# A written-out instruction order with another rule for VectorE's masks, other ranks, and one weight load split (DeltaNet, then a mixture of experts)

## The chip, the cores and the metric

The kernel runs on one core of one Trainium2 chip. The metric is the device time of one launch in microseconds (us). Three runs of the kernel before gave 531.04, 532.78 and 533.56 us, the median is 532.78 us.

## What is computed

The first half is DeltaNet attention: 4 batches of 8 heads, 768 steps, 48 features. The second half sends each of the 3072 rows of the result (384 features) to one of 8 experts. Cut to what matters:

```python
k_n = k / (norm(k) + 1e-6)
for t in range(S):                                # S = 768
    y[:, :, t] = q_t @ state                      # the state before the step
    v_old = k_t @ state
    state += beta_t * outer(k_t, v_t - v_old)
x = y.transpose(0, 2, 1, 3).reshape(B * S, H * D)
logits = x @ w_gate                               # 8 experts
expert = argmax(logits); gate = softmax(logits)[expert]
out = gate * (relu(x @ w1[expert]) @ w2[expert])  # w1 384x1024, w2 1024x384
```

## The kernel before

The time steps are cut into 12 tiles of 64 steps. Inside a tile the recurrence is solved at once: products of keys with keys and queries with keys (`scores`), an inverse of a triangular matrix per head (`invert`, one for each pair of tiles, numbers 0 to 5), and a chain on TensorE that carries the state on (`turn`). In detail:

- `scores(t)` runs 32 or 64 small matmuls into a PSUM pair, ScalarE copies the results to `XY` and to `Pm(t)`. Then VectorE multiplies `Pm(t)` by a fixed 0/1 pattern (L412, 128x1024). This multiplication is called the mask of tile t here. For tiles 0 and 1 the diagonal blocks `GD` are copied straight from PSUM in four quarters each (L311 on VectorE, L309 on ScalarE); later tiles get theirs by a DMA.
- `invert(n)` is VectorE's work: two block transposes (L437), a chain of some 17 tiny operations of 32 columns that forms the norms (L445 to L470, each needs the one before), one scaling (L476), 16 elimination steps (L486 to L498), a first transpose back (L517), 16 more steps (L504, L509) and a second transpose back (L517). It serves tiles 2n and 2n+1.
- `turn(t)` takes the values scaled by the norms, applies the inverse twice (L583, with L593 between) and makes the next state (L607). TensorE and ScalarE take turns in it: each matmul group waits for a ScalarE copy of the one before. `output(t)` adds the state's part (L554) and the masked part (L639, this needs the mask of tile t), `logits(t)` transposes the result and multiplies it by the gate's weights (L659, L669, L678).
- `route(m, part)` does the argmax, the softmax and the counting for a group of row tiles. The groups are row tiles 0-7, 8-15, 16-17, 18-21 and 22-23. Its part 1 begins with `rk` (L752), which reads a count made by TensorE (L743, L747), and has `su` (L766), which reads an exponential from ScalarE (L722).
- `listed` makes the lists of rows per expert for tiles 0-17, then 18-21, then 22-23: VectorE builds comparisons (L796, L800, L804), TensorE multiplies them (L812), one more matmul (L817) and a copy give `lst` (L821). From it `numbered` makes `rows_ei`. GpSimd then gathers 256 early rows of expert 0 (L886), TensorE transposes them (L927), and the first expert matmul (L945) begins with 256 rows.
- The experts follow one another: `turned_rows` (L927), `hidden` (L945), `second` (L977), with a short matmul for a remainder (L1025). Weights are loaded by SyncE's queue in order, three 512 KB parts of w1 and two 768 KB parts of w2 for each expert (`weights`).

The order of instructions on each engine isn't the order of the code. Every piece of work is handed to `Plan.op` with its engine, an assumed cost, what it reads and writes, and a rank (`prio`; smaller is more urgent). `Plan.order` walks through time with these assumed costs: on each engine that comes free it picks the ready piece with the smallest rank, and waits for a piece of rank -70 or less if that comes ready within the time of the one picked. It also places filler matmuls (L1120) into pauses of TensorE [...], as many as `ENOUGH` allows in a window. What comes out is one fixed list per engine, run in order. The constants at the head of the file are ranks and assumed costs: `RUN` for scores, `OUT`, `LOG`, `LATER`, `OUTL` for outputs and logits, `LISTS`, `L3`, `L4` for the lists, `VP` for the scaling of values (L530), `MASK` for the masks. An inverse n has rank 2n - 4 (number 0: -80), the mask of tile t has rank t - MASK.

Of the kernel before, what the change touches and what calls it, by code (L numbers as in the profile page):

```python
# [20 lines left out]
NT = S // C  # L21
# [7 lines left out]
NK = DM // 128  # L29
# [4 lines left out]
FAR = 1 << 20  # L34
RING = 6
AHEAD = 5
RUN = 4.75
PAGE, FILL, STALL = 125, 3.8, 0.8
OUT, LOG = 1.1, 0.2
LATER, OUTL = 8, 1.3  # L40
LISTS, L3, L4, TURN = 9.5, 20.2, 11.05, 11.0
APART = 5
VP, MASK = 0.5, 2.2
WINDOW, WAKE, STAY, PASS = 3.413, 1600, 1750, 8.5
FILLER, ENOUGH, FROM = 0.22, 2500, 36.0
SLACK = 2.0
URGENT = -70


class Plan:  # L50
# [37 lines left out]
    def order(self):  # L88
        n = len(self.ops)
        self.all = list(self.ops)  # L90
        recent, emptied, fills, last = [], {}, [], False
        users = [[] for _ in range(n)]
        left = [len(o[3]) for o in self.ops]
        for i, o in enumerate(self.ops):
            for d, lat in o[3]:
                users[d].append((i, lat))
        ready = [0.0] * n
        free = {}
        wait = {}
        page, filled = 0, 0.0  # L100
        window, used, fast = 0, {}, False
        for i, o in enumerate(self.ops):
            if not left[i]:
                wait.setdefault(o[0], []).append(i)
        start, fin = [0.0] * n, [0.0] * n
        done = 0

        def stall(j, t):

            cost, passes = self.ops[j][1], self.ops[j][5]  # L110
            if page + passes < PAGE or not passes:
                return 0.0
            return max(0.0, filled - t - cost / passes * (PAGE - page))

        while done < n:
            best = None
            for e, lst in wait.items():
                if not lst:
                    continue
                f = free.get(e, 0.0)  # L120
                t = max(f, min(ready[i] for i in lst))
                if best is None or t < best[0]:
                    best = (t, e)
            t, e = best
            lst = wait[e]
            i = min(
                (j for j in lst if ready[j] <= t + 1e-9),
                key=lambda j: (self.ops[j][4] + STALL * stall(j, t), j),
            )

            soon = [j for j in lst if self.ops[j][4] <= URGENT and t < ready[j] < t + self.ops[i][1] - 0.05]
            if soon and self.ops[i][4] > URGENT:
                i = min(soon, key=lambda j: ready[j])
                t = ready[i]
            lst.remove(i)
            eng, cost, _, _, _, passes, _, use, cold, pairs = self.ops[i]
            start[i] = t

            f = free.get("PE", 0.0)
            last |= 30 < self.ops[i][4] < 90  # L140
            while eng == "PE" and not last and FROM < f < t - FILLER - 0.05:
                recent = [x for x in recent if x[0] > f - WINDOW]
                b = [b for b in (1, 2) if emptied.get(b, 0.0) <= f]
                if not b or sum(x[1] for x in recent) >= ENOUGH:
                    break
                fills.append((f, len(self.all)))
                self.all.append(("PE", FILLER, self.filler(b[0]), [], 99.0, 2, None, 256, 2.0, {b[0]}))
                recent.append((f, 273))
                w = int(f / WINDOW)
                used[w] = used.get(w, 0.0) + 273  # L150
                page = (page + 2) % PAGE
                f += FILLER
            if passes:
                recent.append((t, use + PASS * passes))
            if passes:

                while int(t / WINDOW) > window:
                    fast = used.get(window, 0.0) >= (STAY if fast else WAKE)
                    window += 1
                if not fast:  # L160
                    cost *= cold
                for k in range(8):
                    w = int((t + cost * k / 8) / WINDOW)
                    used[w] = used.get(w, 0.0) + (use + PASS * passes) / 8
            end = t
            if passes:
                each = cost / passes
                while passes:
                    k = min(passes, PAGE - page)
                    end += k * each  # L170
                    passes -= k
                    page += k
                    if page == PAGE:
                        page = 0
                        end = max(end, filled)
                        filled = end + FILL
            else:
                end += cost
            free[e] = fin[i] = end
            if e != "PE":  # L180
                for b in pairs:
                    emptied[b] = max(emptied.get(b, 0.0), end + self.LAT[e])
            done += 1
            for u, lat in users[i]:
                ready[u] = max(ready[u], end + lat)
                left[u] -= 1
                if not left[u]:
                    wait.setdefault(self.ops[u][0], []).append(u)
        self.start, self.fin = start + [t for t, _ in fills], fin + [t + FILLER for t, _ in fills]
        return [i for _, i in sorted([(start[i], i) for i in range(n)] + fills)]  # L190
# [28 lines left out]
def tile_kernel(ctx: ExitStack, tc: tile.TileContext, kq, ktok, vtok, betal, wgk, w1, w2, out):  # L219
    nc = tc.nc  # L220
    P = Plan()
# [8 lines left out]
    fc, where = _consts()  # L230
# [31 lines left out]
    def kb(b):  # L262
        return [("bk", b), ("bk", b + 1)]
# [23 lines left out]
    GD = blk(8)  # L287
# [7 lines left out]
    def dma(eng, o, i):  # L295
        return lambda: eng.dma_start(out=o, in_=i)
# [19 lines left out]
    P.op("DVE", 0.1, lambda: nc.vector.memset(tiny[:], 0.0), w=["tiny"], prio=-99)  # L316
    P.op("ACT", 0.2, lambda: nc.scalar.activation(out=tiny[:], in_=tiny[:], func=AF.Copy), w=["tiny"], prio=-45)
    P.op("ACT", 0.5, dma(nc.scalar, bl[:], betal), w=["bl"], prio=-49, lat=2.5)
    P.op("ACT", 0.5, dma(nc.scalar, cf[:], nc.inline_tensor(fc, name="c_f32").ap()), w=["cf"], prio=-48, lat=2.5)
    P.op("DVE", 0.2, lambda: nc.vector.memset(wg[:], 0.0), w=["wg"], prio=-48)  # L320
    P.op("ACT", 0.5, dma(nc.scalar, wg[:, :, 0:E], wgk), w=["wg"], prio=-40, lat=2.5)
    P.op("DVE", 1.0, lambda: nc.vector.memset(pairs[0][:], 0.0), w=kb(BS), prio=-50)
# [40 lines left out]
    def scores(t):  # L363
# [16 lines left out]
        if t < 2:  # L380
# [1 line left out]
            P.op("PE", 1.15, lambda: run(b, (0,), range(FQ)), r=kKQ(t, (0,)), w=kb(b), prio=t - 95, passes=64, use=770)  # L382

            for q in range(4):
                eng = ("ACT", "DVE")[u]
                o = GD[quad(q), :, 16 * u : 16 * u + 16].rearrange("p c (e f) -> p c e f", e=2)
                i = pairs[b // 2][quad(q)].rearrange("p e (f c) -> p c e f", c=C)[:, 32 * (q % 2) : 32 * (q % 2) + 32]
                P.op(eng, 0.5 if u == 0 else 0.6, copy(eng, o, i), r=kb(b), w=[("GD", q, u, e) for e in range(2)], prio=t - 94)
            P.op("ACT", 1.0, copy(
                "ACT",  # L390
                xy[:, :, 16 * u : 16 * u + 16].rearrange("p c (e f) -> p c e f", e=2),
# [446 lines left out]
            a[:, NK * F :].rearrange("p (c d) -> p c d", c=NF),  # L838
        )

    def weights(e, pr, behind=()):
        i = e % 3
        a1, a2 = wview(i)
        extra = []
        if e == 0:
            extra = kXY(0) + kXY(1) + [("GL", k) for k in range(2)]
        if e == 1:
            extra = [("P", k) for k in range(RING)]
        if e == 2:
            extra = [k for i in range(2) for k in (("U", i), ("U", i, 21))] + [("GD", q, u, e) for q in range(4) for u in range(2) for e in range(2)] + kXY(2)  # L850
            extra += [("TT", k, h) for k in range(2) for h in range(2)]
        for s in range(NK):
            P.op("SP", SP(524288),
                 dma(nc.sync, a1[:, s, :], w1[e].rearrange("(s p) f -> p s f", p=128)[:, s, :]),
                 r=behind, w=[("w", i, s)] + extra, prio=pr + s)
        for h in range(2):
            P.op("SP", SP(786432),
                 dma(nc.sync, a2[:, 4 * h : 4 * h + 4, :],
                     w2[e].rearrange("(c p) d -> p c d", p=128)[:, 4 * h : 4 * h + 4, :]),
                 r=behind, w=[("w", i, 3 + h)] + extra, prio=pr + 3 + h)  # L860
# [128 lines left out]

    def early_rows():  # L990

        weights(0, 8)
        prepare(0)
        two_tiles = lst[:].rearrange("p (t e) o -> p t e o", e=E)[:, 0:2, 0, :]
        numbered(rows_ei[:], two_tiles[:, :, 0], "rows_ei", ["lst"], -74)
        dve(2, lambda: nc.vector.tensor_copy(out=rows_e[:], in_=two_tiles[:, :, 1]), ["lst"], ["rows_e"], -73)
        xv = XIN[0][0]
        for t in range(2):
            P.op("POOL", 1.0, lambda t=t: gather(xv[:, t * DM : t * DM + DM], rows_ei[:, t : t + 1]),
                 r=["rows_ei"] + [("xs", i) for i in range(18)], w=[("xin", 0, t)], prio=11, lat=2.5)  # L1000
# [87 lines left out]
                last_rows()  # L1088
    prepare(1)
    numbered(rows_i[:], lst[:, :, 0], "rows_i", ["lst"], -74)  # L1090
    early()

    weights(1, 20, ["rows_i"])
# [125 lines left out]
```

## Time and profile before

| what | value |
|---|---|
| median of three runs | 532.78 us |
| the profiled execution's own time | 526.99 us |
| its span, first to last instruction | 525.2 us |
| TensorE busy | 468.0 us (89%), mean granted clock 0.952 |
| VectorE busy | 243.7 us (46%) |
| ScalarE busy | 191.0 us (36%) |
| GpSimd busy | 84.9 us (16%) |

The profile is of one execution, and its time lies 5.79 us under the median of the runs. In rows of the timeline the columns are start, duration, engine, line of the code, operation, tiles out<-in, and in brackets the idle time before it and what ended it. A row of windows gives for each engine the busy microseconds, then the granted clock of TensorE as a share of full speed, the DMA share and GB/s. The share of busy time hides that the launch has two halves. In the first, up to about 220 us, VectorE is busy nearly all the time until 186 us. In the second, TensorE is.

### The profile page before, as it was taken

What the parts mean: (1) busy time and instruction counts of PE and PEld (TensorE: products, weight loads), DVE (VectorE), ACT (ScalarE), POOL (GpSimd) and SP (SyncE); (2) the same over time, 40 slices, a digit from 0 to 9 for tenths busy, and PEclk for the clock granted to TensorE, in tenths of its full rate; (3) what the DMA queues carried; (4) which work ended last, traced back from release to release, by engine and by line L of the source; (5) the groups of instructions that cost most, each with busy time, mean ns of one, the idle gap of its engine ahead of it and who ended that gap; (6) DMA issues with size and microseconds to landing.
All of it is one profiled execution on the core that took longest, in us unless ns stands there. A gap on an engine that the chain in (4) does not pass through costs nothing. (4 is left out here: it accounts for less than half of the span.)

```text
span 525.2 us, 15838 instructions
## 1 busy us (share of the span) xinstructions
PE 468.0 (89%) x6850; PEld 321.4 (61%) x6851; DVE 243.7 (46%) x958; ACT 191.0 (36%) x452; POOL 84.9 (16%) x91
## 2 busy tenths in 40 slices
PE   5668898888897898999999999999999999999991
PEld 3557787776786786875755555555555555555550
DVE  3999989999699973251303012212030220121210
ACT  2494978888569974510110110010100111100100
POOL 9100000000010010006510321402301302011020
PEclk9556999899999999999999999999999999999996
DMA  8987365364342434395543413612532301000000
GB/s 202 222 211 201 118 164 161 94 150 131 101 134 94 134 115 152 100 385 176 177 175 121 150 54 139 193 34 107 196 120 82 126 4 46 0 18 30 0 31 13
DMA packets 27849, 63.84 MB, mean 122 GB/s; under 512 B 4026, under 2 KB 16220, under 8 KB 27744
## 3 DMA queue, kind: packets, MB, share of 16 engines
q1 hardware_dynamic: 23376, 52.44, 32.9%
q0 software_dynamic: 3584, 9.44, 5.5%
q10 hardware_dynamic: 816, 0.92, 0.8%
q8 instruction: 54, 0.88, 0.7%
q14 instruction: 19, 0.16, 0.1%
HBM read 49.67 MB, written 11.01 MB: 116 GB/s over the span
## 5 line engine op out<-in xcount | busy, mean ns | idle before, releaser
L945 PE MATMUL pair<-kqA,blkA 128*128 128x416 f32 (+2 forms) x288 | 86.9, 458 | 0.0
L977 PE MATMUL pair<-blkA,kqA 128*128 128x384 f32 x240 | 79.0, 489 | 0.0
L951 DVE TENSOR_SCALAR kqA<-pair 128x416 f32<-128x416 f32 (+2 forms) x36 | 19.6, 543 | 121.7 <-PE pair L945 121.7
L945 PEld LDWEIGHTS pair<-kqA,blkA 128*128 128x128 f32 x288 | 51.2, 190 | 31.3 <-issue 28.3
L977 PEld LDWEIGHTS pair<-blkA,kqA 128*128 128x128 f32 x240 | 45.1, 190 | 33.3 <-issue 3.1
L893 POOL DMA_INDIRECT out<-y,rows_i x30 | 28.7, 956 | 199.7 <-DVE y L1038 122.1
L954 ACT ACTIVATE kqA<-pair 128x416 f32<-128x416 f32 (+2 forms) x36 | 17.2, 478 | 108.9 <-PE pair L945 108.9
L968 ACT ACTIVATE y<-pair,lst 128x384 f32<-128x384 f32 x15 | 8.7, 581 | 128.0 <-PE pair L977 118.3
L373 PE MATMUL pair<-kqA 48*64 48x128 f32 (+1 forms) x896 | 36.3, 319 | 17.4 <-ACT blkA L309 6.0
L945 PE MATMUL pair<-kqA,pA 128*128 128x416 f32 x144 | 51.0, 513 | 0.0
L530 ACT ACTIVATE v<-v,nt 128x48 f32<-128x48 f32 x192 | 48.9, 329 | 3.4 <-DMA v<-in_vtok 1.9
L977 PE MATMUL pair<-pA,kqA 128*128 128x384 f32 x144 | 47.2, 488 | 0.0
L373 PEld LDWEIGHTS pair<-kqA 48*64 48x64 f32 x896 | 29.9, 176 | 23.4 <-ACT pA L309 7.9
L554 PE MATMUL pair<-S,kqA 112*64 112x96 f32 x704 | 35.7, 253 | 9.5 <-ACT S L309 3.1
L945 PEld LDWEIGHTS pair<-kqA,pA 128*128 128x128 f32 x144 | 27.1, 190 | 22.5 <-issue 21.6
L977 PEld LDWEIGHTS pair<-pA,kqA 128*128 128x128 f32 x144 | 27.1, 190 | 20.1 <-issue 1.9
L554 PEld LDWEIGHTS pair<-S,kqA 112*64 112x64 f32 x704 | 30.8, 138 | 12.5 <-issue 4.7
L886 POOL DMA_INDIRECT kqA<-xs,rows_i x30 | 29.8, 994 | 43.2 <-DVE more L1115 26.7
L583 PE MATMUL pair<-R,blkA 32*32 32x48 f32 x1536 | 28.6, 226 | 3.0 <-ACT R L309 1.8
L965 DVE TENSOR_SCALAR y<-pair,lst 128x384 f32<-128x384 f32 x7 | 4.3, 618 | 55.3 <-PE pair L977 55.3
L583 PEld LDWEIGHTS pair<-R,blkA 32*32 32x32 f32 x1536 | 25.3, 146 | 7.3 <-ACT R L309 3.8
L490 DVE TENSOR_TENSOR prod<-blkA 128x16 f32<-128x16 f32 (+7 forms) x96 | 28.8, 300 | 0.0
(136 smaller groups left out, 615.6 us busy)
## 6 DMA issues: line engine op xcount, KB each, us to landing
kqA<-in_kq SPq DMA_DIRECT2D x46, 192.0 KB, 5.2
blkA<-in_w SPq DMA_DIRECT2D x15, 512.0 KB, 4.9
blkA<-in_w SPq DMA_DIRECT2D x10, 768.0 KB, 5.5
v<-in_vtok SPq DMA_DIRECT2D x12, 384.0 KB, 4.1
kt<-in_ktok SPq DMA_DIRECT2D x12, 384.0 KB, 3.6
xs<-x SPq DMA_DIRECT2D x12, 384.0 KB, 2.9
pA<-in_w SPq DMA_DIRECT2D x9, 512.0 KB, 5.6
pA<-in_w SPq DMA_DIRECT2D x6, 768.0 KB, 4.7
```

Of the source, the lines that this page charges most:

```text
L373: nc.tensor.matmul(bk[bank + e][half(x), i * w : i * w + w].rearrange("p (k c) -> p k c", c=C), lhsT=v[feat(e), 0, x * FQ + f, :], rhs=v[f ...
L490: dve(16 * w, lambda j=j, w=w, pl=pl: nc.vector.tensor_tensor(out=pl, in0=gl[:, 16:32, j : j + 1].to_broadcast([128, 16, w]), in1=u[:, j : ...
L530: P.op("ACT", 0.225, lambda v=v, i=i: nc.scalar.activation(out=v, in_=v, func=AF.Copy, scale=nt[:, 16 * u + i : 16 * u + i + 1]), r=[("nt" ...
L554: nc.tensor.matmul(bk[bank + g][half(x ^ g if first else x), 2 * D * i : 2 * D * i + 2 * D], lhsT=KQ(t)[0 : 64 + D, k, x * FQ + f, :], rhs ...
L583: nc.tensor.matmul(at(BZ, f, e)[quad(q)], lhsT=tt[quad(q), :, 16 * u + 8 * e + f], rhs=R[quad(q), f, e, :], start=True, stop=True, skip_gr ...
L886: nc.gpsimd.indirect_dma_start(out=dst, out_offset=None, in_=xs, in_offset=bass.IndirectOffsetOnAxis(ap=idx, axis=0), bounds_check=N - 1, ...
L893: nc.gpsimd.indirect_dma_start(out=out, out_offset=bass.IndirectOffsetOnAxis(ap=idx, axis=0), in_=src, in_offset=None, bounds_check=N - 1, ...
L945: nc.tensor.matmul(bk[b][:, 0:n], lhsT=a1[:, s, f * 128 : f * 128 + 128], rhs=xT[:, s, :], start=(s == 0), stop=(s == NK - 1))
L951: (lambda f=f, b=b: nc.vector.tensor_scalar(out=hT[:, f, :], in0=bk[b][:, 0:n], scalar1=0.0, scalar2=None, op0=OP.max))
L954: (lambda f=f, b=b: nc.scalar.activation(out=hT[:, f, :], in_=bk[b][:, 0:n], func=AF.Relu)),
L968: (lambda: nc.scalar.activation(out=y[0:n], in_=bk[b][0:n, 0:DM], func=AF.Copy, scale=gate)),
L977: nc.tensor.matmul(bk[b][:, 0:DM], lhsT=hT[:, f, at : at + 128], rhs=a2[:, f, :], start=(f == 0), stop=(f == NF - 1))
```

## The change

Six things change; the parts that only move line numbers are left out. In `Plan.order` a rule is added for VectorE: before the piece picked is begun, a piece that is more urgent by over 0.5 and comes ready within `NEAR` (0.3 us, and within the piece's own cost) is waited for. Ranks and `ENOUGH` are changed. The constants' load is told to the planner as landing after 8.5 us in place of 2.5 us. One of the four copies of `GD` for tile 1 moves from VectorE to ScalarE. The two w2 loads of expert 0 are handed over later, with rank 18 to 19 behind the last tile's second result. The order is then made anew from all this, so that pieces not named here also change places.

```diff
-RUN = 4.75
+RUN = 4.5
-OUT, LOG = 1.1, 0.2
-LATER, OUTL = 8, 1.3
-LISTS, L3, L4, TURN = 9.5, 20.2, 11.05, 11.0
+OUT, LOG = 0.6, 0.9
+LATER, OUTL = 7, 1.1
+LISTS, L3, L4, TURN = 10.4, 11.0, 11.05, 11.0
-VP, MASK = 0.5, 2.2
+VP, MASK = 1.5, 1.5
-FILLER, ENOUGH, FROM = 0.22, 2500, 36.0
-SLACK = 2.0
+FILLER, ENOUGH, FROM = 0.22, 2300, 36.0
+NEAR, SLACK = 0.3, 2.0
...
+            elif e == "DVE":
+
+                soon = [j for j in lst if self.ops[j][4] < self.ops[i][4] - 0.5
+                        and t < ready[j] < t + min(self.ops[i][1] - 0.05, NEAR)]
+                if soon:
+                    i = min(soon, key=lambda j: (self.ops[j][4], ready[j]))
+                    t = ready[i]
...
-    P.op("ACT", 0.5, dma(nc.scalar, cf[:], nc.inline_tensor(fc, name="c_f32").ap()), w=["cf"], prio=-48, lat=2.5)
+    P.op("ACT", 0.5, dma(nc.scalar, cf[:], nc.inline_tensor(fc, name="c_f32").ap()), w=["cf"], prio=-48, lat=8.5)
...
-                eng = ("ACT", "DVE")[u]
+                eng = "ACT" if u == 0 or q == 3 else "DVE"
...
-                P.op(eng, 0.5 if u == 0 else 0.6, copy(eng, o, i), r=kb(b), w=[("GD", q, u, e) for e in range(2)], prio=t - 94)
+                P.op(eng, 0.6 if eng == "ACT" else 0.7, copy(eng, o, i), r=kb(b), w=[("GD", q, u, e) for e in range(2)], prio=t - 94)
...
-    def weights(e, pr, behind=()):
+    def weights(e, pr, behind=(), of=(0, 1)):
...
-        for s in range(NK):
+        for s in range(NK if 0 in of else 0):
...
-        for h in range(2):
+        for h in range(2 if 1 in of else 0):
...
-        weights(0, 8)
+        weights(0, 8, of=(0,))
...
+    weights(0, 18, [("Z", (NT - 1) % 2)], (1,))
```

## Prediction

> **What bounds the kernel now.** The page names the last chain only for its final 6 us, so I read the slices of the span first, then windows, then each engine's timeline from the start, looking for the place where the second half begins.
>
> ```profile
> DVE  3999989999699973251303012212030220121210
> 350.00:400.00 50.00, 50.00 (x180) 27.67 (x180) 9.05 (x15) 5.25 (x10) 9.79 (x10) 1.00 0.35 123
> 450.00:500.00 50.00, 49.32 (x174) 26.79 (x173) 10.44 (x18) 4.78 (x9) 3.78 (x4) 1.00 0.04 13
> ```
>
> From the first expert matmul at 219.72 us TensorE is nearly full at full clock: between there and 513 us its idle pieces are 0.98, 0.39, 0.84, 1.18, 1.18 and 0.68 us, 5.3 us in all. Its order and work there are kept by the change but for a few swaps in the first 17 us. So the end moves with the start of that matmul. Ahead of it VectorE is 90% full up to 186 us. It matters where its inverses begin and end:
>
> ```profile
> 10.71 0.22 ACT L309 ACTIVATE ents<-cf 128x24 f32<-128x24 f32 x1 [6.54 <-DMA cf<-c_f]
> 13.24 1.30 DVE L437 STREAM_TRANSPOSE blkA<-blkA 128x512 f32<-128x512 f32 x2 [2.14 <-ACT blkA L309]
> 39.20 0.71 DVE L517 STREAM_TRANSPOSE blkA<-blkA 128x512 f32<-128x512 f32 x1
> 72.21 0.70 DVE L517 STREAM_TRANSPOSE blkA<-blkA 128x512 f32<-128x512 f32 x1
> 136.50 0.22 DVE L766 TENSOR_REDUCE su<-ex 128x8 f32<-128x64 f32 x1 [4.82 <-ACT ex L722]
> 185.49 0.71 DVE L517 STREAM_TRANSPOSE blkA<-blkA 128x512 f32<-128x512 f32 x1
> 193.40 0.55 DVE L796 TENSOR_TENSOR ones_p<-cf,places_f 128x384 f32<-128x384 f32 x1
> ```
>
> ScalarE stands 6.54 us for the constants, with the copies that the first inverse needs behind it. Inverse 0 runs from 13.24 to 39.91, inverse 1 ends at 72.91 and inverse 5 at 186.20. The list begins at 193.40. VectorE stood 4.82 us in the middle of inverse 4. The last stretch decides when the experts begin:
>
> ```profile
> 206.82 0.43 PE L817 MATMUL pair<-cf,lstT 128*128 128x64 f32 x2
> 208.81 1.19 POOL L886 DMA_INDIRECT kqA<-xs,rows_ei  x1 [13.61 <-DVE rows_ei L830]
> 215.65 0.63 PE L927 MATMUL pair<-cf,kqA 128*128 128x128 f32 x4
> 219.72 1.56 PE L945 MATMUL pair<-kqA,blkA 128*128 128x256 f32 x6
> ```
>
> The list's last matmul to the first expert matmul is 12.9 us: list, gather, transposes, with the last turn beside it.
>
> [...] a 128x32 operation is 0.19 us, a 128x256 one 0.42, and in a chain the next starts 0.22 to 0.24 us after the last. [...] Here the clock is 0.50 in 96 to 98 us after four thin microseconds, and 64 matmuls of L583 take 1.51 us instead of 1.13. [...] The early gathers here land 3.5 us after issue. [...] L465 took 1.09 us beside a GpSimd memset where it takes 0.18 later; I let that stand, since both move forward together.
>
> **The change, part by part.** I compared the order of instructions on each engine with the order before.
>
> *Start.* The copy of the constants now stands behind the five quarter copies on ScalarE. Those need 5 x 0.58 us from about 6.9, so they end at 9.8. VectorE keeps three of its four copies of 0.70 us from 8.31 and ends at 10.4. The first transpose goes at 10.45 instead of 13.24: -2.8 us. The cover for the moved quarter is ScalarE, idle there before; without it VectorE would end at 11.1.
>
> *Inverses.* An inverse alone costs 39.91 - 13.24 - 0.9 (the L465 case) = 25.8 us. A mask costs 1.11 to 1.18 us start to start, 2.3 for two. The order now reads: inverse 0, masks 0 to 2, inverses 1 and 2, masks 3 and 4, inverse 3, masks 5 and 6, inverse 4, masks 7 and 8, inverse 5, masks 9 and 10, route group 1 with mask 11 inside, group 2, lists. Before, masks 0 to 5 (7.2 us) all lay in or ahead of inverse 1. Ends, in us: inverse 0 at 37.1 (39.91 before), 1 at 37.1 + 3.4 + 25.8 = 66.3 (72.91), 2 at 92.1, 3 at 120.2. Group 0's first 14 small operations stay alternated with inverse 4's chain: 14 such pairs took 3.39 us, 0.24 a pair, hardly more than the chain alone; all of group 0 adds 1.2. So inverse 4 ends at 120.2 + 2.3 + 25.8 + 1.2 = 149.5 plus its waits.
>
> *The wait in inverse 4.* The 4.82 us stall was for an exponential that ScalarE did late. Now the exponential is still behind turn 6's first copies, and `rk` stands only 8 operations behind `su`, where 25 inverse operations lay between. `rk` needs TensorE's count, which before ended 1.0 us ahead of turn 6 (139.99 against 140.99). VectorE gets there at about 129.5. Turn 6 by the turn chain: turn 2 at 67 instead of 77.27, turn 3 at 80.3 (13.3 later, as before), turn 4 behind mask 3 (ready 93.3) with L639, L554, logits and scores, 98.7. Then some 15 and 17 us as before less waits that go: 131. The count ends at 130: I charge 1.0 us, with 0 and 4.8 as bounds. Inverse 4 ends at 150.5, inverse 5 at 150.5 + 2.3 + 25.8 = 178.6.
>
> *From inverse 5 to the list.* Before, groups 1 and 2 ran alternated with each other and with the inverse's end: 7.2 us from 186.20 to 193.40. Now they stand in single file: masks 9 and 10 2.3, group 1 part 0 14 x 0.22 = 3.1, mask 11 1.1, part 1 8 x 0.22 = 1.8, group 2 8 x 0.22 = 1.8, its count on TensorE 0.9, the rest alternated with the list's head 1.4. That is 12.4, so the list starts at 191.0: 2.4 us early. Of 7.6 us gained at inverse 5's end, 5.2 are given back.
>
> *The list.* Six rounds of three comparisons have 0.47 + 0.28 + 0.36 = 1.11 us each, 6.7 us. Waits on L812 were 1.80, 0.58 and 1.43, and 2.66 passed from the copy of `lstT` (204.16) to L817, TensorE being in a group of L554 with a hole of 1.52. Now the six products are spread between turn 10, turn 11 and the logits, and inverse(11) stands just ahead of L817. Turn 10 can't go before group 1's count, about 185. Placing them one by one: waits of 1.6, 1.0 and 0.4 in the rounds, then 0.9 and 0.7. Total 11.3 against 13.4: L817 at 191.0 + 11.3 = 202.3, 4.5 us early.
>
> *After that.* Gathers, transposes and the last output keep 12.9 us, so the expert matmul starts at 215.2. The w2 loads of expert 0, two of 768 KB, move from 197.5 to behind output 10's store, about 207. They land 5.5 us after issue by the page, some 214; their user starts 17.1 us after the first expert matmul, at 232. Cost nothing; without that cover it would be their lateness. On SP only the last stores and the next weights (needed at 259) stand behind them. The gathers are issued first[...]. Fillers fall from 46 to 29. They fill pauses, so they save nothing on the path [...].
>
> **Sum.** -2.8 (start), -3.8 (inverse 4's wait, 4.8 to 1.0), -1.6 (a VectorE wait for mask 7 at 75.78 that goes), +3.7 (inverses now pay their own pauses: (172.96 - 22.1 for masks, routing and waits) / 6 = 25.1 before, 25.8 now), +2.1 (routing in single file, the remainder), -2.1 (list) = -4.5 us. Span 525.2 - 4.5 = 520.7, and 1.8 around it gives 522.5 against 526.99 of the profiled execution. The runs' median lies 5.8 us above it, so I take 532.78 - 4.5 = 528.3 us.
>
> **The rivals.**
> - *The list is not the gate, turn 11 is.* Its first matmul was 210.66 and by my placing is 200.9, 9.8 us early. If the list keeps up (routing nearer 8 us than 12), the experts start 9 us early: 523.8. For it: turns 7 to 9 have slack of 2 to 3 us. Against: the single file is in the order.
> - *All given back.* If the list's rounds lose what they lost before (13.4) and the turns slip 2 us, -0.4: 532.4. For it: holes of 1.3 to 1.5 us in TensorE (L593, L554) that no wait explains and that can fall anywhere.
> - *Slower, by the clock and `rk`.* TensorE stands up to 4 us for mask 3 at about 89 to 93, with fewer fillers. [...] if turn 6 slips from 131 to 139 VectorE stands 8 us at `rk`, which moves all behind it: 7 us past my sum of 1.0, +2.5 net, 535.3. It decides once turn 6 starts later than about 136. For it: the same place lost 4.82 before. Against: 5 us of slack to that point.
> - *The rule does not do what it says*: ruled out by the order, where masks stand between inverses.
>
> **Chances.** A measurement of this kernel can tell 0.5%, 2.7 us. Forecast case 0.52 (525.5 to 530.6), of which 0.04 falls within 0.5%; turn 11 as gate 0.20; given back 0.14; slower 0.14. Faster 0.68, same 0.18, slower 0.14. The range 522.5 to 534.0 leaves out the best part of the second case and the bad part of the last.
>
> **What would show it.** L437 first at 10.4 to 10.6; ends of L517 at 37, 66, 92, 120, 150 and 178.6; masks between; no stall over 2 us at `su` or `rk`; first L796 at 191; L817 at 202; first L945 at 215; no idle in TensorE before L977 for w2. It is wrong if inverse 5 ends after 183, or if L945 follows L817 by more than 14 us.

## The result, and the profile after

The changed kernel took 533.67 us (median of 19 runs) against 531.04 us for the kernel before beside it (19 runs). The ratio of the two is 1.0068, 95% interval [1.0041, 1.0095]: slower by 0.68%. The forecast was 528.3 us, faster by 0.85%.

The profiled execution of the changed kernel took 536.10 us, its span is 534.3 us. That is 9.1 us above the profiled execution of before, more than the ratio says, so the landmarks below overstate the loss. The kernels of one experiment ran beside the kernel before on one chip, and different experiments ran on different chips (the kernel before had medians from 529.79 to 537.59 us). So ratios are compared below, not times. A ratio depends a little on the chip too: from the first expert matmul to the end, profiles of the changed order show 303.7 to 303.9 us where the kernel before had a median below 533 us, and 306.9 to 309.8 us on the two chips where it had 537; those of the old order show 305.3 to 305.5 and 310.4 to 311.7 us.

| us from the span's start | forecast | before | changed |
|---|---|---|---|
| end of inverse 0 | 37.1 | 39.91 | 37.00 |
| end of inverse 1 | 66.3 | 72.91 | 66.04 |
| end of inverse 3 | 120.2 | 127.5 | 119.6 |
| end of inverse 5 | 178.6 | 186.20 | 190.00 |
| turn 2 | 67 | 77.27 | 72.1 |
| turn 6 | 131 | 140.99 | 142.84 |
| turn 10 | 185 | 193.7 | 201.72 |
| list begins | 191.0 | 193.40 | 207.51 |
| first expert matmul | 215.2 | 219.72 | 230.55 |
| from there to the end | 305.5 | 305.5 | 303.8 |

Where the changed profile answers to the lines shown of before: first the slices of VectorE and a window of the second half (columns: length, PE, PEld, DVE, ACT, POOL, clock, DMA share, GB/s).

```profile
DVE  4999999995499966254223012212021220121110
...
450.00:500.00 50.00, 49.32 (x165) 27.34 (x164) 7.79 (x13) 5.77 (x11) 4.75 (x5) 1.00 0.05 18
```

The second half is as full as before, and the loss lies ahead of it. In the changed kernel's code the lines below L135 lie 7 further on (L583 is L590), in the experiments further still (L610 or L603 for L583, L580 for L554, L620 for L593, L634 for L607, L667 for L639, L707 for L678, L838 for L812). Now the timeline of ScalarE, then that of VectorE.

```profile
23.91 0.33 ACT L537 ACTIVATE v<-v,nt 128x48 f32<-128x48 f32 x1 [6.31 <-DMA v<-in_vtok]
```

```profile
11.05 1.30 DVE L444 STREAM_TRANSPOSE blkA<-blkA 128x512 f32<-128x512 f32 x2
...
65.33 0.71 DVE L524 STREAM_TRANSPOSE blkA<-blkA 128x512 f32<-128x512 f32 x1
...
118.88 0.71 DVE L524 STREAM_TRANSPOSE blkA<-blkA 128x512 f32<-128x512 f32 x1
...
140.16 0.22 DVE L773 TENSOR_REDUCE su<-ex 128x8 f32<-128x64 f32 x1 [11.69 <-ACT ex L729]
...
142.55 0.23 DVE L759 TENSOR_TENSOR rk<-pair,cnt 128x72 f32<-128x72 f32 x1 [1.20 <-PE pair L754]
...
189.29 0.71 DVE L524 STREAM_TRANSPOSE blkA<-blkA 128x512 f32<-128x512 f32 x1
...
201.44 0.23 DVE L759 TENSOR_TENSOR rk<-pair,cnt 128x72 f32<-128x72 f32 x1 [5.13 <-PE pair L754]
...
207.51 1.32 DVE L803 TENSOR_TENSOR ones_p<-cf,places_f 128x384 f32<-128x384 f32 x1
```

Up to 119.6 us VectorE did what was forecast, within 0.6 us. The wait for the constants on ScalarE is gone, but ScalarE now stands 6.31 us for the values of the next tile, with the copies of scores behind it. From 128.5 us VectorE stands 11.69 us at `su`, in inverse 4, and later 5.13 us at the `rk` of group 1. This looks like the cause. It is not, as the first experiment shows. The end of the first half:

```profile
219.05 0.43 PE L824 MATMUL pair<-cf,lstT 128*128 128x64 f32 x2
...
221.04 1.19 POOL L893 DMA_INDIRECT kqA<-xs,rows_ei  x1 [12.23 <-DVE rows_ei L837]
...
230.55 1.56 PE L952 MATMUL pair<-kqA,blkA 128*128 128x256 f32 x6
```

From the list's last matmul to the experts it is 11.5 us, 12.9 before. So the loss was there at the list, and ahead of it at turn 10. What TensorE did from turn 9 to turn 10, before and then in the changed kernel:

```profile
180.84 1.13 PE L583 MATMUL pair<-R,blkA 32*32 32x48 f32 x64 [0.16 <-ACT R L309]
...
183.97 0.39 PE L678 MATMUL pair<-cf,lgT 64*128 64x8 f32 x4
...
193.69 1.13 PE L583 MATMUL pair<-R,blkA 32*32 32x48 f32 x64
```

```profile
184.59 1.13 PE L590 MATMUL pair<-R,blkA 32*32 32x48 f32 x64 [0.49 <-ACT R L316]
...
187.72 0.39 PE L685 MATMUL pair<-cf,lgT 64*128 64x8 f32 x2
191.03 0.38 PE L685 MATMUL pair<-cf,lgT 64*128 64x8 f32 x2 [2.93 <-issue]
...
192.49 1.51 PE L590 MATMUL pair<-R,blkA 32*32 32x48 f32 x64
...
201.72 0.50 PE L590 MATMUL pair<-R,blkA 32*32 32x48 f32 x19
```

Two windows of it (columns as above):

```profile
188.00:191.00 3.00, 0.10 (x1) 0.01 (x1) 2.93 (x12) 1.53 (x2) 0.00 (x0) 0.93 0.16 60
191.00:197.00 6.00, 5.97 (x130) 5.38 (x133) 4.90 (x17) 0.99 (x2) 0.00 (x0) 0.50 0.02 3
```

In the middle of a group of four logits matmuls, which ran through before, TensorE stands 2.93 us for "issue", nothing that a semaphore explains. It was busy for 0.10 us between 188 and 191 us. After that the same 64 matmuls of L590 take 1.51 us in place of 1.13: the clock is at half speed (0.50 from 190.6 to 197.4 us), a cold stretch; in the 3.41 us ahead of it TensorE was busy for 0.95 us. This turn takes 17.1 us; before it took 12.9. The waits of TensorE between 38 and 236 us, by line (us in total, times, longest):

```profile
PE pair L600 <- issue: 5.3, 5, 1.6
...
PE pair L646 <- issue: 4.0, 3, 2.0
...
PE pair L685 <- issue: 2.9, 1, 2.9
```

All holes put down to "issue" in this stretch sum to 16.8 us in the changed kernel and to 8.2 us before. The part of the page on DMA queues (packets, MB, share of 16 engines) has a line, the same before and after, that I had passed over:

```profile
q8 instruction: 54, 0.88, 0.7%
```

54 transfers, in the trace of 16,384 bytes each. TensorE has 13,633 matmuls and weight loads in the trace, about 252 for each such transfer. I take each for the fetch of a block of TensorE's instructions, 256 to a block (the power of two next above 252): a reading of these numbers, which experiment 3 tests. To see whether the holes lie at the heads of blocks, I counted TensorE's instructions in order of start up to each hole, and took the remainder by 256. Ten of the eighteen holes:

```
hole ends at (us)   length   instruction   remainder
 76.21               1.54       2983          167
 94.90               1.65       4003          163
109.42               0.30       4769          161
122.34               0.54       5534          158
127.17               0.65       5790          158
130.62               0.16       6046          158
136.64               2.04       6301          157
166.33               1.41       8087          151
191.03               2.93       9365          149
211.00               1.08      10387          147
```

In 17 of the 18 holes the remainder lies on one line that drifts slowly from 176 to 146 (semaphore instructions and lost records aren't counted). The holes stand at the heads of blocks, whatever instruction is there, and end 1.25 to 1.55 us after a block has landed. For the block of the 2.93 us hole: the one ahead of it began to run at 184.81, the fetch began only at 188.6, landed at 189.6, and the block ran at 191.03. Of the 42 fetches between 38 and 236 us 23 begin 0.5 to 1.5 us after the block ahead of them begins to run.

### The profile page after: what moved, and what is told of

It reads as the page before. It is cut to its first block, busy times and chain, and to the rows that moved or that the text cites. A ratio compares the mean times of both kernels' runs of the same rounds, so it can differ in the third digit from the quotient of the medians.

```text
span 534.3 us, 15773 instructions
## 1 busy us (share of the span) xinstructions
PE 468.0 (88%) x6816; PEld 321.8 (60%) x6817; DVE 246.9 (46%) x957; ACT 191.8 (36%) x453; POOL 84.8 (16%) x91
## 5 line engine op out<-in xcount | busy, mean ns | idle before, releaser
L961 ACT ACTIVATE kqA<-pair 128x416 f32<-128x416 f32 (+2 forms) x36 | 17.1, 478 | 109.2 <-PE pair L952 109.2
L590 PE MATMUL pair<-R,blkA 32*32 32x48 f32 x1536 | 30.1, 229 | 4.2 <-ACT R L316 2.9
L590 PEld LDWEIGHTS pair<-R,blkA 32*32 32x32 f32 x1536 | 26.3, 147 | 9.2 <-ACT R L316 5.2
```

The costliest lines, as they stand in the source:

```text
L590: nc.tensor.matmul(at(BZ, f, e)[quad(q)], lhsT=tt[quad(q), :, 16 * u + 8 * e + f], rhs=R[quad(q), f, e, :], start=True, stop=True, skip_gr ...
L961: (lambda f=f, b=b: nc.scalar.activation(out=hT[:, f, :], in_=bk[b][:, 0:n], func=AF.Relu)),
```

## The experiments

Four theories are told apart here (the expectations below name others where they come up): V, VectorE's stall at `su` and `rk` sets the end. T, the chain of turns on TensorE and ScalarE sets it. P, what slows that chain is where TensorE's instructions stand in the blocks. L, the large holes come where a block's fetch meets large transfers.

All edits are made in the finished order: `seqs` holds the list of each engine, and instructions are moved or put in before they are recorded.

**1. The stall taken away.**

```diff
+        q = seqs['DVE']
+        su = [i for i in q if note(i) == ('su', 0)]
+        rk = [i for i in q if note(i) == ('rk', 0)]
+        q = [i for i in q if i not in su + rk]
+        i4 = [i for i in q if note(i) == ('inv', 4)]
+        k = q.index(i4[88]) + 1
+        q[k:k] = rk
+        k = q.index(i4[-1]) + 1
+        q[k:k] = su
```

> The changed kernel, with one thing moved: the three operations on su of route group 0 stand behind inverse 4, and rk with its four followers stands some 85 operations into inverse 4, where TensorE has its count ready. VectorE should then not stand still in inverse 4. Theory T (the chain of turns on TensorE and ScalarE sets the pace, VectorE is ahead of it): inverse 5 ends near 178 us instead of 190, turn 10 still begins at 198 to 202, and the time stays within 1.5 us of the changed kernel's, a ratio to the kernel before of 1.003 to 1.009. Theory V (the 11.7 us wait of VectorE is what costs): turn 10 and the first expert matmul come 5 to 10 us earlier, ratio 0.985 to 0.997.

Measured 1.014 [1.0087, 1.0194], above what either theory allowed. VectorE no longer stands, neither at `rk` nor at `su`:

```profile
143.60 0.23 DVE L783 TENSOR_TENSOR rk<-pair,cnt 128x72 f32<-128x72 f32 x1
...
150.01 0.17 DVE L798 TENSOR_REDUCE su<-ex 128x8 f32<-128x64 f32 x1
```

Inverse 4 ends at 150.1 in place of 161.7 us, inverse 5 at 184.9 in place of 190.0, and nothing behind them comes earlier: turn 6 at 143.9, turn 10 at 202.8, the first expert matmul at 233.6. V falls. Why this run was even slower than the changed kernel stays open; it ran on one of the two slower chips.

**2. Parts of the change, one by one.**

More fillers in turns 1 to 5, three ahead of each L614:

```diff
+        for t in range(1, 6):
+            kz = [i for i in q if note(i) == ('turn', t)][-1]
+            k = q.index(kz)
+            for j in range(3):
+                P.all.append(('PE', FILLER, P.filler(1), [], 99.0, 2, None, 256, 2.0, {1}))
+                q.insert(k, len(P.all) - 1)
```

> The changed kernel with 15 more filler matmuls, three ahead of the state matmuls (L614) of turns 1 to 5 each, where TensorE waits about 1 us for ScalarE's copy anyway. Theory C (fewer fillers let the clock fall[...]): mean granted clock rises from 0.936 to 0.945 or more, at most 3 cold stretches between 50 and 230 us where the changed kernel had 5, and the ratio falls from 1.007 to about 1.001. Theory T without the clock: no change beyond 1 us, ratio 1.005 to 1.009, or 1 to 2 us more for the slots that the fillers take.

Measured 0.9909 [0.988, 0.9938], but not for the reason given: the clock was 0.941, below what was expected of more fillers (0.936 in the changed kernel, where between 50 and 230 us it is 0.50 from 77.9 to 84.8, 95.0 to 98.4 and 190.6 to 197.4 us, five times 3.41 us; what such stretches cost in the ratio was the author's estimate), and turn 6, behind the fillers, came at 141.6, only 1.2 us earlier. Most of the gain came at once between turns 9 and 10, 11.5 us in place of 17.1, where no filler had been added. Fifteen fillers are 60 instructions (two matmuls and two weight loads each), so everything behind them stands 60 places further on in the blocks. This is where P came from.

The rule taken out, all else kept, order anew:

```diff
-            elif e == "DVE":
+            elif e == "DVE" and NEAR:
-NEAR, SLACK = 0.3, 2.0
+NEAR, SLACK = 0.0, 2.0
```

> The changed kernel with the new rule for VectorE switched off, all other edits kept, order made anew: masks 3 to 5 stand in the first part of inverse 1 again, masks 9 to 11 ahead of inverse 5. If the rule is what costs: ratio to the kernel before 0.995 to 1.000. If the other edits (ranks, fewer fillers) cost: 1.004 or more. Under theory T the rule itself moves little: within 2 us of the changed kernel.

Measured 1.004 [1.0017, 1.0064]. So there is a loss without the rule too. The order anew also changes the number of fillers, so this run mixes the rule with the places; it says no more.

The start alone, in the kernel before (the constants' 8.5 us and the quarter of `GD`):

```diff
-name="c_f32").ap()), w=["cf"], prio=-48, lat=2.5)
+name="c_f32").ap()), w=["cf"], prio=-48, lat=8.5)
-                eng = ("ACT", "DVE")[u]
+                eng = "ACT" if u == 0 or q == 3 else "DVE"
```

> The kernel before with the two edits of the start alone: the constants' load told as 8.5 us, and one quarter of tile 1's diagonal blocks copied by ScalarE. Inverse 0 should end 2.5 to 3 us earlier, near 37.2 us. Theory V (VectorE's chain is passed on to the end): ratio 0.993 to 0.996, 2 to 3.5 us. Theory T (the turns set the pace): turn 0 may begin up to 2 us earlier, but the time stays within 0.3%, ratio 0.997 to 1.003.

Measured 0.9966 [0.9942, 0.999], between the ranges of the two theories. Inverse 0 ended at 37.1, 2.8 us early as forecast, but inverse 1 at 76.1 and turn 10 at 194.8, both later than in the profile of before. Two fillers more in the new order move places here too. What the start alone is worth stays open.

The tail of the order put right, on top of the fillers of e2_fillers (masks 9 to 11 ahead, group 2's first part ahead of group 1's second, TensorE's counts one place earlier):

```diff
+        late = {t: [i for i in q if note(i) == ('mask', t)] for t in (9, 10, 11)}
+        k = q.index([i for i in q if note(i) == ('su', 0)][0])
+        q[k:k] = late[9] + late[10]
+        k = q.index([i for i in q if note(i) == ('inv', 5)][2])
+        q[k:k] = late[11]
+        two = [i for i in q if note(i) == ('route', 2, 0)]
...
+        k = q.index([i for i in q if note(i) == ('route', 1, 0)][-1]) + 1
+        q[k:k] = two
```

> The changed kernel with the 15 fillers in turns 1 to 5, and its tail put right: masks 9 and 10 stand in front of su in inverse 4, where VectorE waits anyway, mask 11 behind inverse 5's second transpose, group 2's first part ahead of group 1's second, and TensorE's two counts each one place earlier, as in the kernel before. Theory R (routing in single file behind masks after inverse 5 makes the list late against turn 10): the first comparison comes 3 to 5 us earlier against turn 10, the first expert matmul 2 to 4 us earlier, ratio 0.983 to 0.988. If the list isn't the gate there: 0.989 to 0.994, as with the fillers alone.

Measured 0.9959 [0.9936, 0.9981], no better than e2_fillers and above both ranges. The list began 6.8 us after turn 10, in e2_fillers 5.8: the moves bought nothing.

**3. The places alone.** Fifteen fillers ahead of turn 0, spread over the groups of scores there, in the changed kernel and in the kernel before; then eight in the changed one:

```diff
+        for op, n in zip(q[4:11], (2, 2, 3, 2, 2, 2, 2)):
+            for j in range(n):
+                P.all.append(('PE', FILLER, P.filler(1), [], 99.0, 2, None, 256, 2.0, {1}))
+                q.insert(q.index(op), len(P.all) - 1)
```

> The changed kernel with 15 more fillers, all of them in the scores ahead of turn 0, where TensorE stands 1.1 us between groups; no filler is added in the turns. They only move all later instructions of TensorE on by 60 places. Theory P (TensorE's instructions come in blocks of 16 KB, and where in the turns a block ends decides how long it stands; the changed order happened to get a bad place, the 2.9 us hole in L685 of turn 9 with a cold stretch behind it): that hole goes or shrinks below 1 us, turn 9 to turn 10 takes 11 to 14 us instead of 17, and the ratio to the kernel before is 0.988 to 0.999, as with the 15 fillers in turns 1 to 5 (0.991). Theory C (fillers help because they keep the clock up in turns 1 to 5): ratio 1.005 to 1.012, with the hole where it was.

> The kernel before with the same 15 fillers ahead of turn 0. Theory P: the time moves by some 0.3% or more, up or down, though nothing else changed; since the kernel before has few holes (7 us in all between 38 and 236 us), up is likelier, ratio 1.002 to 1.012. Without theory P: the fillers lie in pauses, ratio 0.998 to 1.002.

> The changed kernel with 8 early fillers, half of the shift. Theory P: the hole in turn 9 moves or shrinks in part; a time between the changed kernel and the one with 15, or another place that is hit, ratio 0.990 to 1.008. Theory C: no change, 1.005 to 1.010.

Measured 0.9889 [0.9858, 0.992] for the changed kernel with 60 places, 1.0133 [1.0093, 1.0172] for the kernel before with the same 60, 0.9929 [0.9904, 0.9953] for the changed kernel with 32. That is what P wanted, 1.0133 being a little above its range. The same addition speeds one kernel up by 1.8% and slows the other by 1.3%. But fillers also are work, and the mean granted clock of the profiled execution was 0.955 with the fifteen early ones and 0.936 without. So the same places were filled with small matmuls, 32x32 on 32x48, and once with 64 of them, 256 instructions, one whole block:

```diff
+        pad = lambda: nc.tensor.matmul(
+            pairs[1][0:32, 1, DM : DM + 48], lhsT=const("ident")[0:32, 0:32], rhs=const("ident")[0:32, 0:48],
+            start=False, stop=True, skip_group_check=True)
```

> The changed kernel with 15 small matmuls (32x32 on 32x48, four instructions each, 60 in all) in the places where e5_shift15 had its 15 large ones: the same 60 places in the stream of instructions, but hardly any TensorE work. Theory P (TensorE's stream is fetched in blocks of 256 instructions, and the time hangs on which instruction stands at the head of a block): a ratio to before as that of e5_shift15, 0.986 to 0.995, and no hole of more than 1.5 us at the logits of turn 9. Theory C (the large matmuls helped because they kept the clock up and TensorE warm): as the changed kernel, 1.003 to 1.010, with the hole of nearly 3 us at L685's instruction back.

> The changed kernel with 64 small matmuls early, 256 instructions, one whole block: every later instruction stands at its old place in a block. Theory P: as the changed kernel, 1.003 to 1.011, and the hole at the logits of turn 9 is back at 2 us or more. Theory C (more early work is better) : at or below e9_after_pad60, and under 0.997.

> The kernel before with the 60 places of small matmuls. Theory P: as e6_before15, slower than before by 0.8 to 1.7 per cent. Theory C (the large early matmuls themselves delayed the kernel before): [...] the loss goes, within 0.4 per cent of before.

> The kernel before with 256 places of small matmuls, one whole block. Theory P: back to before, within 0.4 per cent (0.996 to 1.004). Theory C: the more early instructions the worse, 1.010 or more.

| instructions put in early | 0 | 60 | 256 |
|---|---|---|---|
| changed kernel | 1.0068 | 0.9847 [0.9791, 0.9903] | 1.0072 [1.0041, 1.0103] |
| kernel before | 1 | 1.0101 [1.0057, 1.0144] | 1.0004 [0.9974, 1.0033] |

Small work does what large work did (mean granted clock 0.947 with the 60 places), and a whole block brings both kernels back to where they were, though it is more work than the 60: P is shown. (0.9847 lies a little below P's range.) The profiles say it too. TensorE in turn 9 with 60 places, and then with 256:

```profile
183.81 0.39 PE L707 MATMUL pair<-cf,lgT 64*128 64x8 f32 x4
...
184.87 1.13 PE L610 MATMUL pair<-R,blkA 32*32 32x48 f32 x64
...
192.42 0.78 PE L610 MATMUL pair<-R,blkA 32*32 32x48 f32 x40
```

```profile
191.28 0.38 PE L707 MATMUL pair<-cf,lgT 64*128 64x8 f32 x2
194.32 0.28 PE L707 MATMUL pair<-cf,lgT 64*128 64x8 f32 x2 [2.65 <-issue]
...
195.17 1.28 PE L610 MATMUL pair<-R,blkA 32*32 32x48 f32 x64
```

With 60 places the four logits matmuls run through, the clock stays at 1.00 from 180 to 197 us, and turn 10 follows turn 9 after 11.7 us. With 256 the hole is back in the same place, between the second and the third of them. In the kernel before 60 places put a block's head into the list's products:

```profile
208.39 0.43 PE L838 MATMUL pair<-ones_p,vals 128*64 128x128 f32 x3
212.65 0.69 PE L838 MATMUL pair<-ones_p,vals 128*64 128x128 f32 x3 [3.83 <-issue]
```

From the list's first comparison to its last matmul it took 18.4 us there, 13.4 before. The block ahead of this one began to run at 205.69 us and the fetch only at 210.22: from 205 to 210.4 us the transfer engines are at nine tenths or more (but for 0.6 us at six to eight tenths), with two 768 KB loads of w2 sent from 204.22 us.

**4. What the change is worth without this luck.** Shifts by 128 and 192 places were added for both kernels.

> The changed kernel with 128 places (32 small matmuls) early: half a block. Theory F (the change itself is worth about the 0.85 per cent of the forecast, and its place in the blocks hid it): the mean ratio of the changed kernel over the four shifts 0, 60, 128 and 192 lies 0.5 to 1.3 per cent below the mean of the kernel before over the same four shifts; for this run alone 0.985 to 1.010. Theory G (the change is worth nothing, only the place in the blocks decides): the two means lie within 0.3 per cent.

> The changed kernel with 192 places early, three quarters of a block. Theory F: mean over four shifts 0.5 to 1.3 per cent below that of the kernel before; alone 0.985 to 1.010. Theory G: the two means within 0.3 per cent, so this one and e13_after_pad128 near 1.005 and above.

> The kernel before with 128 places early. Both theories: between 0.997 and 1.016, as its place in the blocks decides; theory F wants the mean over the four shifts (1.000, 1.010, this one, the next) at 1.003 or more.

> The kernel before with 192 places early. Both theories: between 0.997 and 1.016; theory G wants the mean over the four shifts no more than 0.3 per cent away from that of the changed kernel.

| places | 0 | 60 | 128 | 192 | mean |
|---|---|---|---|---|---|
| changed | 1.0068 | 0.9847 | 0.9891 [0.9854, 0.9928] | 0.9995 [0.9969, 1.0021] | 0.9950 |
| before | 1 | 1.0101 | 1.0003 [0.9982, 1.0024] | 0.9988 [0.9967, 1.0009] | 1.0023 |
| difference | +0.0068 | -0.0254 | -0.0112 | +0.0007 | -0.0073 |

The means lie 0.73% apart, the forecast was 0.85%. But the four differences spread over 3.2%, so the standard error of their mean is about 0.7% (their standard deviation of 1.4%, halved for four), as large as the mean itself, and the pairs come from three experiments. Theory F also wanted 1.003 or more as the mean of the kernel before; it is 1.0023. This points to a gain by the change itself and doesn't show it.

**5. Why some holes are long.** In the changed kernel the first two of three 512 KB loads of w1 go out at 183.62 us, and the block ahead of the 2.93 us hole begins to run at 184.81, when the fetch of the next one is due. In one run these two alone were moved on SyncE, behind the next load of `kt`; TensorE's places stay.

```diff
+        q = seqs['SP']
+        two = [i for i in q if note(i) == ('w', 0)][:2]
+        q = [i for i in q if i not in two]
+        k = q.index([i for i in q if note(i) == ('w', 0)][0])
+        q[k:k] = two
```

> The changed kernel with the first two w1 loads of expert 0 moved behind the load of kt for tile 11 on SyncE, from 183.6 us to about 198 us; every other engine's order and every place in the blocks is as in the changed kernel. Theory L (the block of instructions ahead of the logits of turn 9 came 5 us late because its fetch stood in the transfers of those two loads): the hole of 2.93 us there falls to 1.5 us or less, the cold stretch at 190 us goes, turn 10 begins 3 to 6 us earlier against turn 9 (12 to 14 us after it, not 17.1), and the ratio to before falls to 0.995 to 1.003, unless the loads delay another block after 198 us. Theory N (the transfers have nothing to do with it): the hole stays at 2 us or more and the ratio at 1.003 to 1.011.

> The same move in e9_after_pad60, where no block's head lay in the time of the loads. Theory L: little to win, 0.982 to 0.992 as that kernel; if the loads now meet the fetch of a block after 195 us, up to 0.995. Theory N: as that kernel, 0.980 to 0.990.

Measured 1.0005 [0.9985, 1.0026], from 1.0068. The loads go out at 193.5 us, and turn 9's logits and the matmuls of turns 9 and 10 are now:

```profile
188.96 0.39 PE L707 MATMUL pair<-cf,lgT 64*128 64x8 f32 x4
...
190.02 1.13 PE L610 MATMUL pair<-R,blkA 32*32 32x48 f32 x64
...
197.35 1.13 PE L610 MATMUL pair<-R,blkA 32*32 32x48 f32 x64
```

The same window in the changed kernel and in this run, with the DMA share and GB/s at its end:

```profile
183.60:188.80 5.20, 4.01 (x149) 3.23 (x148) 5.20 (x27) 4.25 (x12) 0.00 (x0) 1.00 0.84 280
```

```profile
183.60:188.80 5.20, 5.20 (x150) 4.23 (x148) 5.13 (x27) 3.60 (x8) 0.00 (x0) 0.65 0.23 79
```

The fetch of the same block began 0.28 us after the block ahead of it began to run, in place of 3.83 us; turn 10 follows turn 9 after 12.2 us. L holds for this hole, and moving the two loads, and with them this hole and its cold stretch, took away about the whole loss against the kernel before (0.63%, from two experiments). A stretch at half clock lay at 180.5 us in this run instead (0.66 in the mean from 179 to 183.6 us), beside another wait (2.48 us for a ScalarE copy, until 180.94). In the kernel with 60 places the same move costs: 0.9968 [0.9943, 0.9994] against 0.9847 (0.9889 with fillers), measured on other chips and a little more than I had expected at most. There the loads go out from 190 us on, and two blocks that had been free now have holes:

```profile
200.37 0.38 PE L580 MATMUL pair<-S,kqA 112*64 112x96 f32 x2 [0.95 <-issue]
...
203.83 0.31 PE L667 MATMUL pair<-Z,pA 64*64 64x48 f32 x2 [0.94 <-issue]
```

The fetch for the first began 3.6 us after the block ahead (197.96 against 194.4), in the transfers. That for the second began 1.1 us after, when the loads were over, so only the first is a case of L. Together they are 0.36% of the time, and the rest of this loss isn't explained.

The builds with the old order hold further cases. In all seven the fetch that falls into the transfer of expert 0's two w2 loads (sent at 197.5 us in the kernel before) begins 2.7 to 5.1 us after the block ahead, and a hole of 1.5 to 3.8 us follows, 1.52 us in the kernel before. In all thirteen builds with the changed order those loads go out later (226.2 us in the changed kernel), and there is no hole over 1.4 us between 195 us and the first expert matmul. So moving w2 seems to take a hole away, which the prediction didn't foresee; no run moved these loads alone.

**A version that beats both** is the changed kernel with 60 places put in early: 0.9847 with small matmuls, 0.9889 with fillers. 128 places do as well, 0.9891.

## Why the prediction was wrong

*VectorE's part was right.* The start brought 2.2 us of the 2.8 forecast at the first transpose and 2.9 at inverse 0's end. Inverses 0 to 3 ended within 0.6 us of the working, masks standing between them as read from the order.

*The step that failed* is the turn chain: "turn 2 at 67 instead of 77.27, turn 3 at 80.3 (13.3 later, as before)", then 98.7, and turn 6 at 131. Turn 6 came at 142.84, 1.9 us later than before. Two things were wrong in it.

First, turn 2 was tied to the end of inverse 1. It had to wait for turns 0 and 1 and the matmuls that stand ahead of it on TensorE: turn 0 began at 40.9 though inverse 0 had ended at 37.0, since ScalarE's 6.31 us stand for values made the scores late (TensorE waited 5.47 us for a copy of theirs until 25.27), and two turns then took 31.2 us. The new rank `VP` makes these values more urgent; that it put them ahead of the copies is read from the order, and no run changed `VP` alone. With the inverses early, TensorE's chain became the limit: from turn 1 to turn 2 its waits are for ScalarE's copies and for "issue", none for VectorE. In none of the runs with the changed order did turn 2 begin before 70.5. That VectorE was 90% full had been taken for proof that the turns would follow it.

Second, the turns' lengths were carried over from before as if they belonged to the work. From turn 2 to turn 6 the forecast had 64 us, as before (63.7); it took 70.7, and with 60 places 66.1. From turn 6 to turn 10 it took 58.9, before 52.7, and with 60 places 53.0. These lengths contain the fetch holes and cold stretches (in the changed kernel holes of 1.54, 1.65 and 2.93 us end at 76.2, 94.9 and 191.0 us, and the clock is 0.50 from 77.9, 95.0 and 190.6 us), and removing 17 fillers of four instructions and swapping groups moved every block's head. The second rival had the sign of it, "holes of 1.3 to 1.5 us in TensorE (L593, L554) that no wait explains and that can fall anywhere", but made nothing more of it than the gain given back (-0.4 us net). The trace of before held what was needed: 8 of its 9 holes, those of L593 and L554 among them, already lay at the heads of blocks (remainders from 178 to 152).

*"Fillers fall from 46 to 29; they save nothing on the path"* took them for work only. They are also instructions, and their number sets the place of all that follows: 60 places were worth 2.2% in this kernel.

*The wait at `su` and `rk`* was forecast at 1.0 us and was 12.9. The forecast had VectorE there at 129.5 and it came at 128.5, but turn 6 was 12 us late. The size was wrong because of the chain; it cost nothing, as experiment 1 shows. So the rival "slower, by the clock and `rk`" had the right side and the wrong mechanism: turn 6 was past 136 us as it required (its slip to 139 had been the author's estimate), but the stand of VectorE didn't set the end. One of the signs of being wrong that the prediction named did come, inverse 5 ending after 183 us (190.0).

*Routing and list*: from inverse 5's end to the list 17.5 us against 12.4, of which 5.1 is the wait of `rk` for group 1's count, which TensorE makes just ahead of turn 10. The list itself took 11.5 us, forecast 11.3. Here TensorE was late again and not VectorE.

*The w2 loads* cost nothing, as forecast, though they went out at 226.2 us and not at about 207. What was missed in the other direction is 1.7 us after the first expert matmul: the last list's waits on TensorE before (0.98 and 0.39 us) are gone.

*One sum*: the +3.7 for the inverses' own pauses comes to 4.2 by its two figures (six times 25.8 less 25.1). The total doesn't hang on it, since +2.1 is a remainder: 178.6, 12.4, 11.3 and 12.9 give 215.2 us, 4.5 before 219.72.

## What to carry to other kernels

When TensorE runs thousands of small matmuls, count the holes put down to "issue", number the instructions, and see whether they lie 256 apart, as here; if so, a kernel is a draw of block places, and a change of half a per cent can't be judged from one build (60 places moved these two kernels by -2.2% and +1.0%). Build both versions at several shifts (some dummy matmuls early on) and compare the means, and keep large loads out of the time in which a block on the critical path is fetched (worth 0.63% here). And where an engine is nearly full, ask what the chain behind it needs when that engine gets faster, before letting the chain follow it.

## What the runs showed that was not expected

- Fetching TensorE's instructions isn't hidden here. The holes put down to "issue" are up to 3.83 us long and 8 to 18 us in all in 198 us, and nearly all of the long ones stand at the heads of blocks. In the changed kernel a fetch begins 0.5 to 1.5 us after the block ahead begins to run in 23 cases of 42, takes 0.9 to 2.1 us, and where TensorE waits for it the block runs 1.25 to 1.55 us after it has landed. That makes some 2.7 us from head to head at the least, an estimate from the smallest of each. 64 matmuls of L590 with their weight loads take 1.13 us, so a block full of such would be run in 2.3 us, by the same kind of estimate, and the next would have to wait.
- A fetch that met two 512 KB loads began 3.83 us after the block ahead, 0.28 us with the loads moved, and made a hole of 2.93 us. The move was worth 0.63% of the whole time.
- Sixty dummy instructions at the start, hardly any work (64 matmuls of this form with their loads take 1.13 us in the turns), moved the time of one kernel by -2.2% and that of the other by +1.0%; 256 left both as they were.
